# A list scheduler that lets ScalarE and VectorE read the same PSUM banks one after the other

## The chip, the cores and the metric

The kernel runs on one core of a Trainium2 chip. The metric is the device time of one execution in microseconds; the time before is 1328.19 us, the median of three runs (1327.75 to 1329.28).

## What is computed

12480 tokens of 128 channels go through an attention with 49 agents, then through two feed-forward blocks of 2048 hidden channels: the first with silu, the second with a rational function of its hidden value. All in float32; the weights come as float64 and are converted on the chip.

```python
a2k = softmax(agents @ k.T * scale)            # 49 x 12480
agent_v = a2k @ v                              # 49 x 128
x = softmax(q @ agents.T * scale) @ agent_v    # 12480 x 128
h = x @ moe_w_in;  x = (h * sigmoid(h)) @ moe_w_out
h = x @ moe2_w_in
P = a0 + a1 * h + a2 * h**2 + a3 * h**3
Q = 1 + |b0| * |h| + |b1| * h**2
out = (P / (Q + 1e-6)) @ moe2_w_out
```

## The kernel before, in words

The tokens are worked in 25 groups of 512 (the last has 192), a group's hidden channels in 8 pairs of 128-channel blocks. A step has a name, a group `g` and a pair `p`:

- First block: M1 (TensorE, 4 matmuls into an `h` tile of two PSUM banks), S1 (ScalarE, silu from there into an `s` tile), M2 (TensorE, 2 float32 matmuls, each shown as two in the trace, adding into `x2`). After eight pairs XS (VectorE) splits `x2` into `xh` and `xl`.
- Second block: M3 (TensorE, 6 matmuls into an `h` tile). Four steps read that tile: U (z = a3 h + a2; VectorE L550 for pairs 0 to 3, ScalarE L548 for pairs 4 to 7), W1 (VectorE L575, z = z h), W2 (VectorE L579, z = (z + a1) h) and AB (ScalarE L557, m = |h|). N and Q (GpSimd, L563 and L571) make the denominator from `m` in a `y` tile of two pairs; L and R (ScalarE, L584 and L587) turn it into its reciprocal by a logarithm and a sigmoid; G2 (VectorE L591) joins numerator and reciprocal; M4 (TensorE L600) adds up the output, O1 to O3 transpose and store it.
- The queries of two groups together: QT, QTc, QS, QM, QE, QN, QB, QBc, QBl; QT, QS and QB are TensorE's (8 transposes, 16 score matmuls, 8 transposes).
- Ahead of it: k, v, the query and the matrices are loaded by SP's queue in the order of the string `LOADS` (k, v, q; a digit or sign is one of 16 matrix pieces of 512 KB). For each k piece KT, KC, KS, then KV (ScalarE) and KM (VectorE) read the scores; X0 to X2 take the maximum over all 13 pieces; EX, ET, EC, AV follow for each piece, then F0 to F4 and V0 to V2. A matrix piece goes through C0 to C3 (C4, C5), from a `raw` buffer of which there are four.

What limits running ahead: three `h` slots, one `x2` and one `ot` bank, five `s`, thirteen `z`, two `m` and six `y` tiles. An activation table holds silu, logarithm, sigmoid or exponential, and a change is a table load; the four logarithms and four sigmoids of a group run as one batch in which no silu may start.

The order of every engine's instructions is fixed when the program is built. `scheduled` plays the kernel through with a length for each step (`COST`), a time that a result needs to another engine (`TELL`, `TAIL`), and a priority `g + place[0] + place[1] * p / 8` from `PLACE`; it takes on each engine, among the steps that could start within `SLACK` of the soonest, the one with the smallest number. The two readers U and AB of one `h` tile have no dependence on each other in this list: it may place them at the same time. The tile framework, which puts in the semaphores, lets no two engines use the same PSUM bank at once: of two readers on different engines, the second in the program's order waits for the first. An engine's queue is worked in order, so an instruction that waits holds up what stands behind it.

Of the kernel before, what the change touches and what calls it, by code (L numbers as in the profile page):

```python
# [26 lines left out]
NX = 1  # L27
NKV = 11

LOADS = "kkkkk0kkk1kkk2kqk3vv4vv5vv6vv7vv8vv9v:;<=>?"  # L30

# [16 lines left out]
}  # L48
PLACE = {
# [13 lines left out]
}  # L63
SLACK = {"PE": 0, "ACT": 0, "DVE": 0, "POOL": 3.73}
READY_Y = 4
TAIL = {"PE": 0.17, "ACT": 0.125, "DVE": 0.085, "POOL": 0.02, "DMA": 2.0}

# [4 lines left out]

TELL = {
    "PE": {"PE": -0.17, "ACT": 0.04, "DVE": 0.04}, "ACT": {"PE": 0.055, "DVE": 0.035, "POOL": 0.1, "ACT": 0.03},
    "DVE": {"PE": 0.055, "ACT": 0.095, "POOL": 0.1, "DVE": 0.02},
    "POOL": {"ACT": 0.1, "DVE": 0.1, "PE": 0.06, "POOL": 0.06}, "DMA": {"DMA": -2.0},
}
TABLE = {"S1": "silu", "L": "ln", "R": "sigmoid", "QE": "exp", "EX": "exp"}
SWITCH = 1.283

PORT = {"N", "Q", "G2", "QN", "C0", "C2", "C3", "C5"}
H_SLOTS = 3


def group_steps(groups, pairs, part=1.0):
# [16 lines left out]
    last, land = None, {}  # L102
    for i, what in enumerate(LOADS):
        n = count.get(what, 0)
# [101 lines left out]
def buf_counts(n=None):  # L206

    n = n or globals()
    return dict(
        h=n["H_SLOTS"], x2=1, ot=1, s=n["NS"], xh=n["NX"], z=n["NZ"], m=n["NM"], y=n["NY"], oT=1, ob=2,  # L210
        qT=1, e=1, xt=2, kv=NKV, raw=4, kT=2, eT=3, ca=2, cb=3, w2=2,
    )


def scheduled(groups, pairs, part=1.0):

    ops = group_steps(groups, pairs, part)
    bufs = buf_counts()
    free = {tag: [0.0] * n for tag, n in bufs.items()}
    taken = {tag: 0 for tag in bufs}  # L220
    users, last, where = {}, {}, {}
    waits, then = {}, {}
    for k, (_, _, after, _, uses, _) in ops.items():
        for t in uses:
            users[t] = users.get(t, 0) + 1
        waits[k] = len(after)
        for d in after:
            then.setdefault(d, []).append(k)
    at, end = {}, {}
    ready = {e: [] for e in TAIL}  # L230

    def becomes_ready(k):
        at[k] = max([end[d] + TELL[ops[d][0]].get(ops[k][0], 0.1) for d in ops[k][2]], default=0.0)
        ready[ops[k][0]].append(k)

    for k in ops:
        if not waits[k]:
            becomes_ready(k)
    idle = {e: 0.0 for e in TAIL}
    port = {"DVE": 0.0, "POOL": 0.0}  # L240
    table, batch = "exp", None
    n_ln, n_sig = {}, {}
    out = []

    def may_start(k):

        name, g, p = k
        eng, _, _, takes, _, _ = ops[k]
        t = max(idle[eng], at[k])
        for tag, _ in takes:  # L250
            held = free[tag] if tag == "h" else [free[tag][taken[tag] % bufs[tag]]]
            open_ = [x for x in held if x is not None]
            if not open_:
                return None
            t = max(t, min(open_))
        if name in TABLE and name != "R":
            if name == "L":
                if batch not in (None, g) or (batch == g and table != "ln"):
                    return None
                done = sum(all(("Q", g, 2 * h + i) in end for i in (0, 1)) for h in range(4))  # L260
                if batch is None and (p or done < READY_Y):
                    return None
            elif batch is not None:
                return None
        if name == "R" and n_ln.get(g, 0) < 4:
            return None
        if name in PORT:
            t = max(t, port["POOL" if eng == "DVE" else "DVE"])
        return t + (SWITCH if name in TABLE and TABLE[name] != table else 0.0)

    while len(out) < len(ops):
        best = None
        for eng, some in ready.items():
            can = [(t, k) for t, k in ((may_start(k), k) for k in some) if t is not None]
            if can:
                soon = min(can)[0] + SLACK.get(eng, 0.0)
                k = min((ops[k][5], t, k) for t, k in can if t <= soon)
                best = min(best or (1e9,), (k[1], k[0], k[2]))
        t, _, k = best
        name, g, p = k  # L280
        eng, cost, _, takes, uses, _ = ops[k]
        ready[eng].remove(k)
        idle[eng], end[k] = t + cost, t + cost + TAIL[eng]
        if name in PORT:
            port[eng] = max(port[eng], t + cost)
        slot = None
        for tag, what in takes:
            if tag == "h":
                i = slot = min(
                    (i for i, x in enumerate(free["h"]) if x is not None), key=lambda i: free["h"][i]  # L290
                )
            else:
                i = taken[tag] % bufs[tag]
                taken[tag] += 1
            where[what], free[tag][i] = (tag, i), None if users.get(what) else end[k]
        for what in uses:
            users[what] -= 1
            last[what] = max(last.get(what, 0.0), end[k] + 0.06)
            if not users[what] and what in where:
                tag, i = where[what]  # L300
                free[tag][i] = last[what]
        if name in TABLE:
            table = TABLE[name]
            if name == "L":
                batch, n_ln[g] = g, n_ln.get(g, 0) + 1
            elif name == "R":
                n_sig[g] = n_sig.get(g, 0) + 1
                batch = None if n_sig[g] == 4 else batch
        out.append((name, g, p, slot))
        for d in then.get(k, ()):  # L310
            waits[d] -= 1
            if not waits[d]:
                becomes_ready(d)
    scheduled.total = max(end.values())
    return out
# [3 lines left out]
def attention_silu_rational_kernel(  # L319
# [420 lines left out]
    def LD(i):  # L740
        what = LOADS[i]
        if what in "kv":
            load(*((k_t, k) if what == "k" else (v_t, v)))
        elif what == "q":
            q_load(0)
        else:
            job = ord(what) - 48
            load_w(matrices[job // NW], job % NW, job)
        if i == 2:
            nc.sync.dma_start(out=a_sb, in_=ca.partition_broadcast(P))  # L750
            nc.sync.dma_start(out=b_sb, in_=cb.partition_broadcast(P))
# [165 lines left out]
    for name, g, p, slot in scheduled(NG, NP, REST / GW):  # L917
        if late is None and name in ("AB", "U"):
            pre.close()
            late = ctx.enter_context(tc.tile_pool(name="late", bufs=2, reuse_waits="tile"))  # L920
        where = () if slot is None else (slot,)
        if name in steps:
            steps[name](g, p, *where)
        else:
            (one.get(name) or q_steps[name])(g, *where)
# [36 lines left out]
```

## Time and profile before

| | before |
|---|---|
| median of three runs | 1328.19 us |
| profiled execution, device time | 1329.12 us |
| its span | 1327.3 us |
| TensorE, matmuls busy | 1271.6 us (96%) |
| ScalarE busy | 1073.9 us (81%) |
| VectorE busy | 1005.3 us (76%) |
| GpSimd busy | 761.3 us (57%) |
| chain of work that ended last | PE 57%, DVE 23%, ACT 13%, issue 4%, DMA 2% |

The span is the stretch that the profile covers; the device time has 1.8 us around it. In the rows PE is TensorE, PEld its weight load, DVE VectorE, ACT ScalarE, POOL GpSimd, SPq the queue that issues DMAs. `L557` is line 557 of the kernel. A wait is put down to the instruction that released it. Matmuls overlap in the records, and their ends are modelled: a matmul of 0.23 us in the chain is listed with a duration of about 0.39.

### The profile page before, as it was taken

Reading aid. Unit: us, or ns where it says so; the run is one execution under the profiler, and the core shown is the slowest. Engines: PE = TensorE matmul, PEld = TensorE weight load, DVE = VectorE, ACT = ScalarE, POOL = GpSimd, SP = SyncE. Lnnn points to the kernel's source line nnn. Section 1 sums busy time; section 2 is a strip of 40 time slices with the busy share of each in tenths; the row PEclk is TensorE's granted clock in tenths of the full one; section 3 lists DMA queues with packets and bytes.
Section 4 is the critical chain, followed back from the end, with each engine's and each line's share of the span. In section 5 each row is a group of like instructions: output and inputs, shape, how many; then the busy total and the mean of one; then the engine's idle time right before and its main releaser. Section 6 shows DMA issues by size and latency. Waiting matters only on the chain.

```text
span 1327.3 us, 12283 instructions
## 1 busy us (share of the span) xinstructions
PE 1271.6 (96%) x4539; PEld 759.1 (57%) x4539; DVE 1005.3 (76%) x948; ACT 1073.9 (81%) x972; POOL 761.3 (57%) x434
## 2 busy tenths in 40 slices
PE   9899999999999999999999999999999999999987
PEld 5765565555555565565555555555555555555554
DVE  4987778858858787876867858868768769778775
ACT  7686888987996978888787887878878878869876
POOL 2247575556547575484466457556556466575672
PEclk9899999999999999999999999999999999999989
DMA  9720000000000000000000000000000000000000
GB/s 345 280 64 0 17 8 13 12 9 1 24 3 5 24 5 7 21 1 24 9 0 11 22 0 9 24 1 8 21 4 9 3 8 8 9 0 9 8 1 20
DMA packets 14676, 34.77 MB, mean 26 GB/s; under 512 B 1575, under 2 KB 5720, under 8 KB 14616
## 3 DMA queue, kind: packets, MB, share of 16 engines
q1 hardware_dynamic: 14616, 33.98, 7.0%
q8 instruction: 36, 0.59, 0.2%
q14 instruction: 24, 0.20, 0.0%
HBM read 27.59 MB, written 6.39 MB: 26 GB/s over the span
## 4 chain that ended last, share of the span: by engine, by line
PE 57%; DVE 23%; ACT 13%; issue 4%; DMA 2%; POOL 1%; SPq 0%; ACTq 0%; DVEq 0%; POOLq 0%
PE x L516 18%; PE ot L600 13%; DVE z L575 7%; DVE z L579 6%; DVE z L550 6%; PE h L502 5%; PE h L503 5%; PE h L539 5%; ACT m L557 4%; PE h L541 4%; PE h L540 4%; ACT y L584 3%; DVE z L591 3%; ACT z L548 3%; DMA s<-in_k_dram 1%
## 5 line engine op out<-in xcount | busy, mean ns | idle before, releaser
L563 POOL TENSOR_SCALAR y<-m,bab 128x1024 f32<-128x1024 f32 (+1 forms) x200 | 264.4, 1325 | 480.3 <-ACT m L557 462.9
L571 POOL TENSOR_TENSOR y<-y,m 128x1024 f32<-128x1024 f32 (+1 forms) x200 | 468.6, 2358 | 5.2
L516 PE MATMUL x<-s,wo 128*128 128x512 f32 (+1 forms) x800 | 361.9, 581 | 0.4 <-ACT s L509 0.4
L600 PE MATMUL ot<-z,w2o 128*128 128x512 f32 (+1 forms) x800 | 356.7, 588 | 4.4 <-ACT ob L626 2.3
L575 DVE TENSOR_TENSOR z<-z,h 128x1024 f32<-128x1024 f32 (+1 forms) x200 | 237.5, 1191 | 100.3 <-ACT m L557 58.6
L579 DVE SCALAR_TENSOR_TENSOR z<-z,a_sb,h 128x1024 f32<-128x1024 f32 (+1 forms) x200 | 249.5, 1252 | 38.8 <-ACT m L557 34.9
L591 DVE SCALAR_TENSOR_TENSOR z<-z,a_sb,y 128x1024 f32<-128x1024 f32 (+1 forms) x200 | 260.3, 1354 | 19.3 <-ACT y L587 16.6
L557 ACT ACTIVATE m<-h 128x1024 f32<-128x1024 f32 (+1 forms) x200 | 197.8, 1002 | 87.8 <-DVE z L550 44.5
L600 PEld LDWEIGHTS ot<-z,w2o 128*128 128x128 f32 x800 | 150.4, 191 | 159.4 <-issue 145.2
L509 ACT ACTIVATE s<-h 128x1024 f32<-128x1024 f32 (+1 forms) x200 | 196.9, 1004 | 52.1 <-PE h L503 50.0
L516 PEld LDWEIGHTS x<-s,wo 128*128 128x128 f32 x800 | 148.5, 189 | 127.6 <-issue 117.2
L539 PE MATMUL h<-xh,w2l 128*128 128x512 f32 (+1 forms) x400 | 187.1, 468 | 32.0 <-DVE z L579 24.3
L502 PE MATMUL h<-xt,w1a 128*128 128x512 f32 (+1 forms) x400 | 193.0, 484 | 2.7 <-DVE z L579 2.3
L584 ACT ACTIVATE y<-y,eps 128x2048 f32<-128x2048 f32 (+1 forms) x100 | 192.2, 1955 | 0.3
L587 ACT ACTIVATE y<-y 128x2048 f32<-128x2048 f32 (+1 forms) x100 | 181.1, 1862 | 0.3
L548 ACT ACTIVATE z<-h,a_sb 128x1024 f32<-128x1024 f32 (+1 forms) x100 | 118.4, 1184 | 67.9 <-PE h L541 54.2
L550 DVE TENSOR_SCALAR z<-h,a_sb 128x1024 f32<-128x1024 f32 (+1 forms) x100 | 131.1, 1313 | 37.6 <-PE h L541 27.1
L541 PE MATMUL h<-xh,w2h 128*128 128x512 f32 (+1 forms) x400 | 158.9, 397 | 0.0
L540 PE MATMUL h<-xl,w2h 128*128 128x512 f32 (+1 forms) x400 | 158.5, 396 | 0.0
L503 PE MATMUL h<-xt,w1b 128*128 128x512 f32 (+1 forms) x400 | 154.9, 388 | 0.0
L539 PEld LDWEIGHTS h<-xh,w2l 128*128 128x128 f32 x400 | 77.1, 193 | 97.5 <-issue 42.2
L502 PEld LDWEIGHTS h<-xt,w1a 128*128 128x128 f32 x400 | 75.3, 188 | 51.6 <-issue 15.2
(102 smaller groups left out, 866.0 us busy)
## 6 DMA issues: line engine op xcount, KB each, us to landing
q<-in_q_dram SPq DMA_DIRECT2D x12, 512.0 KB, 3.2
out_dram<-ob SPq DMA_DIRECT2D x24, 256.0 KB, 2.0
raw<-in_moe_w_in_dram SPq DMA_DIRECT2D x8, 512.0 KB, 8.7
raw<-in_moe_w_out_dram SPq DMA_DIRECT2D x8, 512.0 KB, 5.9
s<-in_k_dram SPq DMA_DIRECT2D x6, 512.0 KB, 6.5
kv<-in_k_dram SPq DMA_DIRECT2D x6, 512.0 KB, 9.9
s<-in_v_dram SPq DMA_DIRECT2D x6, 512.0 KB, 10.6
kv<-in_v_dram SPq DMA_DIRECT2D x6, 512.0 KB, 9.4
```

What stands on the lines that cost most here:

```text
L502: nc.tensor.matmul(h[:, c, :w], w1a[:, f], xt, start=True, stop=False)
L503: nc.tensor.matmul(h[:, c, :w], w1b[:, f], xt, start=False, stop=True)
L516: nc.tensor.matmul(x2_t[i][:, : cols(i)], wo[:, 2 * p + c, :], s[:, c, : cols(i)], start=(p == 0 and c == 0), stop=(p == NP - 1 and c == 1),)
L539: nc.tensor.matmul(h[:, c, :w], w2l[:, f], xh_t[i], start=True, stop=False)
L557: nc.scalar.activation(m, h2_t[i, p][:, :, : cols(i)], AF.Abs)
L563: nc.gpsimd.tensor_scalar(out=y_t[i, p // 2][:, p % 2], in0=m_t[i, p], scalar1=bab[:, 1:2], scalar2=bab[:, 0:1], op0=ALU.mult, op1=ALU.add,)
L571: eng.tensor_mul(out=y, in0=y, in1=m_t.pop((i, p)))
L575: nc.vector.tensor_mul(out=z, in0=z, in1=h)
L579: nc.vector.scalar_tensor_tensor(out=z, in0=z, scalar=a_sb[:, 1:2], in1=h, op0=ALU.add, op1=ALU.mult)
L584: nc.scalar.activation(y_t[i, h], y_t[i, h], AF.Ln, bias=eps)
L591: nc.vector.scalar_tensor_tensor(out=z, in0=z, scalar=a_sb[:, 0:1], in1=r, op0=ALU.add, op1=ALU.mult)
L600: nc.tensor.matmul(ot_t[i][:, : cols(i)], w2o[:, 2 * p + c, :], z[:, c, :], start=(p == 0 and c == 0), stop=(p == NP - 1 and c == 1),)
```

## The change

- Steps that read the same PSUM tile (`SHARED`: U, AB, W1, W2 of one group and pair; KV and KM of one k piece) are known to the list: a step may not start before the readers of the same tile on another engine have ended, plus the time to tell it. The list chooses other work in the meantime.
- The length of a table change, `SWITCH`, goes from 1.283 to 1.41; the time from the last use of a buffer to its next user from 0.06 to 0.11; `TELL` from VectorE to itself from 0.02 to 0.035.
- All priorities in `PLACE` and the slacks are others (GpSimd's from 3.73 to 10.19, ScalarE's and VectorE's from 0 to 0.1 and 0.11).
- `LOADS` has the k pieces ahead of nearly all else.

No step, tile, buffer count or instruction is changed. The diff, with the table of priorities cut to the steps that the text speaks of:

```diff
-LOADS = "kkkkk0kkk1kkk2kqk3vv4vv5vv6vv7vv8vv9v:;<=>?"
+LOADS = "kkkkkkkk0kkkk1qkv2v3vv4v5vv6v7vv8v9vv:;<=>?"
...
-    "M1": (-0.314, 1.025), "S1": (1.145, 0.916), "M2": (1.021, 0.1), "XS": (-6.422, 0),
-    "M3": (0.964, 0.941), "U": (2.183, 0.836), "W1": (-5.204, 0.983), "W2": (1.364, 0.136),
-    "AB": (2.549, 1.023), "N": (-2.99, 1.223), "Q": (-1.833, 1.4), "L": (5.032, 1.117),
-    "R": (1.379, 0.297), "G2": (1.461, 0.282), "M4": (2.885, 1.172), "O1": (-0.735, 0),
...
+    "M1": (-0.11, 0.763), "S1": (4.253, 0.495), "M2": (2.55, 0.413), "XS": (-10.282, 0),
+    "M3": (0.977, 1.183), "U": (0.653, 0.161), "W1": (2.726, 1.345), "W2": (-4.862, 0.973),
+    "AB": (-4.491, 0.498), "N": (-6.136, 0.226), "Q": (-3.0, 1.078), "L": (6.243, 0.379),
+    "R": (-3.253, 0.354), "G2": (1.443, 0.848), "M4": (4.598, 1.086), "O1": (-0.008, 0),
...
-SLACK = {"PE": 0, "ACT": 0, "DVE": 0, "POOL": 3.73}
+SLACK = {"PE": 0, "ACT": 0.1, "DVE": 0.11, "POOL": 10.19}
...
-    "DVE": {"PE": 0.055, "ACT": 0.095, "POOL": 0.1, "DVE": 0.02},
+    "DVE": {"PE": 0.055, "ACT": 0.095, "POOL": 0.1, "DVE": 0.035},
...
-SWITCH = 1.283
+SWITCH = 1.41
...
+SHARED = {"U": "h", "AB": "h", "W1": "h", "W2": "h", "KV": "k", "KM": "k"}
...
+    seen = {}
...
+        if name in SHARED:
+            for e, x in seen.get((SHARED[name], g, p), {}).items():
+                if e != eng:
+                    t = max(t, x + TELL[e].get(eng, 0.1))
...
+        if name in SHARED:
+            seen.setdefault((SHARED[name], g, p), {})[eng] = end[k]
...
-            last[what] = max(last.get(what, 0.0), end[k] + 0.06)
+            last[what] = max(last.get(what, 0.0), end[k] + 0.11)
```

## Rows read from the trace of the kernel before

**Rows 1.** Page, part 1: busy us (share of the span) xinstructions.
```profile
PE 1271.6 (96%) x4539; PEld 759.1 (57%) x4539; DVE 1005.3 (76%) x948; ACT 1073.9 (81%) x972; POOL 761.3 (57%) x434
```

**Rows 2.** Timeline of VectorE: XS of groups 1, 3, 11, 13 and 23 (start us, us).
```profile
132.02 0.69 DVE L529 CAST xh<-x 128x512 fp32r<-128x512 f32 x1 [2.83 <-PE x L516]
...
228.37 0.68 DVE L529 CAST xh<-x 128x512 fp32r<-128x512 f32 x1
...
624.26 0.69 DVE L529 CAST xh<-x 128x512 fp32r<-128x512 f32 x1 [5.64 <-PE x L516]
...
727.82 0.69 DVE L529 CAST xh<-x 128x512 fp32r<-128x512 f32 x1 [4.44 <-PE x L516]
...
1237.12 0.69 DVE L529 CAST xh<-x 128x512 fp32r<-128x512 f32 x1 [2.54 <-PE x L516]
```

**Rows 3.** Chain of work in order of time, three stretches: start us, us, what.
```profile
444.82 1.73 PE h L440 x16
...
472.99 0.23 PE h L502
...
475.32 1.72 PE x L516 x4
...
624.23 0.87 PE h L422 x8
```

**Rows 4.** Waits of the whole span, TensorE: us in total, times, longest us.
```profile
PE h L539 <- DVE z L579: 24.3, 27, 1.8
```

**Rows 5.** Waits of the whole span, ScalarE and VectorE on AB, U, W1 and GpSimd.
```profile
DVE z L575 <- ACT m L557: 58.6, 58, 2.5
...
ACT m L557 <- DVE z L550: 44.5, 30, 7.9
...
DVE z L579 <- ACT m L557: 34.9, 31, 1.2
...
ACT m L557 <- DVE z L575: 22.6, 35, 3.0
...
ACT m L557 <- POOL y L571: 9.6, 9, 1.2
```

**Rows 6.** Timeline of ScalarE, 629 to 641 us: [idle before <-releaser].
```profile
629.71 1.02 ACT L557 ACTIVATE m<-h 128x1024 f32<-128x1024 f32 x1 [0.93 <-DVE z L550]
...
637.64 1.03 ACT L557 ACTIVATE m<-h 128x1024 f32<-128x1024 f32 x1 [1.13 <-DVE z L550]
...
638.68 1.28 ACT L587 ACT_TABLE_LOAD   x1
...
639.98 1.91 ACT L587 ACTIVATE y<-y 128x2048 f32<-128x2048 f32 x1
```

**Rows 7.** Timeline of TensorE at the same hole.
```profile
641.38 0.47 PE L539 MATMUL h<-xh,w2l 128*128 128x512 f32 x1 [1.84 <-DVE z L579]
```

**Rows 8.** Chain of work in order of time, after the hole.
```profile
643.55 0.43 PE h L540
```

**Rows 9.** Timeline of ScalarE: two silus.
```profile
478.50 1.95 ACT L509 ACTIVATE s<-h 128x1024 f32<-128x1024 f32 x2
```

**Rows 10.** Timeline of VectorE: the last reader of a slot.
```profile
476.64 1.28 DVE L579 SCALAR_TENSOR_TENSOR z<-z,a_sb,h 128x1024 f32<-128x1024 f32 x1 [1.15 <-ACT m L557]
```

**Rows 11.** Chain of work in order of time: the next matmul in that slot.
```profile
477.98 0.50 PE h L502
```

**Rows 12.** Timeline of ScalarE: the first exponential.
```profile
36.16 0.71 ACT L833 ACTIVATE sT<-sT,mx 128x512 f32<-128x512 f32 x1
```

**Rows 13.** Busy us (xinstructions), granted clock and DMA of two stretches.
```profile
core 0: us, PE busy (x) PEld busy (x) DVE busy (x) ACT busy (x) POOL busy (x), PEclk, DMA share, GB/s
...
30.00:45.00 15.00, 11.07 (x72) 8.33 (x69) 13.59 (x29) 13.87 (x34) 4.19 (x3) 0.67 1.05 387
...
1237.00:1328.00 91.00, 74.14 (x277) 45.85 (x275) 64.67 (x68) 68.36 (x67) 46.90 (x34) 0.93 0.03 10
```

**Rows 14.** Waits of SP's queue: us in total, times, longest us.
```profile
SPq L668 <- DVE sb L706: 11.9, 3, 8.6
```

18 rows, old and new, of the table PLACE are left out of this document.

## The prediction

> **What bounds the kernel now.** I read the busy times of the page first [rows 1]. TensorE is busy for 96% of the span, so the kernel looks bound by matmuls with little to win. Ends of matmuls are modelled, though, so the busy share hides short holes. A better measure is the distance between two equal events. XS, the first reader of a finished `x2`, stands once in every group [rows 2]. From group 1 (132.02) to group 23 (1237.12) lie 1105.1 us for 22 groups, which is 100.5 us for two (the query work comes once in two groups). The first such pair, 132.02 to 228.37, took 96.4, a later one, 624.26 to 727.82, took 103.6.
>
> Against that I set what TensorE needs. In a stretch without holes one M1 and one M3 follow each other from 472.99 to 475.32: 2.33 us. M2 takes 1.72 [rows 3], and M4 has the same matmuls. Two groups have 16 pairs: 16 x (2.33 + 1.72 + 1.72) = 92.3. The query steps add 1.73 for QS and 0.87 for eight transposes, twice (QT and QB); O2 is four transposes, 0.44, twice. Together 92.3 + 3.5 + 0.9 = 96.7 us. The excess is 100.5 - 96.7 = 3.8 us in two groups, over eleven of them about 41 us. That is all that a better order can win between group 1 and group 23.
>
> Who makes these holes? Where TensorE stood still, the waits name M3 waiting for DVE L579 (W2), which is the last reader of an `h` tile [rows 4]: all three `h` slots are taken. So I looked at what keeps a slot. After M3, its two banks are read by U, AB, W1 and W2, and in the waits AB (ScalarE) and the three others (VectorE in half of the pairs, U on ScalarE in the other half) wait for each other again and again [rows 5]: 58.6 + 34.9 us on VectorE, 44.5 + 22.6 us on ScalarE, together 160.6 us in 154 waits for 200 pairs. None of these is a need of the data; AB shares nothing with U, W1 and W2 but the bank it reads. The scheduler of before knows nothing of it and places AB beside U, so the instruction that comes second stands at the head of its queue and holds up work that was ready.
>
> One hole shows it [rows 6]: within the logarithms of one group, AB at 629.71 held ScalarE up for 0.93 us until U was done, and AB at 637.64 for 1.13 us again. When M3 began at 641.38, TensorE had stood still for 1.84 us [rows 7], and soon after M3 ran with 0.43 us for a matmul instead of 0.23 [rows 3, 8], the lower of TensorE's two clock levels (1.2 GHz).
>
> **The change, part by part.**
>
> *Readers kept apart.* The removal is in the order, not in the chip's work: no instruction is added or taken away; the same four readers still go one after the other. What can vanish is the head-of-line wait. By the rows above, 160.6 us of such waits go with 41 us of holes: 0.26 us on TensorE for each. The waits on ScalarE (44.5 + 22.6 = 67 us) I take as gone: silu, logarithm and sigmoid work lies ready in most stretches, as around the two waits of the hole above. The waits on VectorE (93.5 us) I take as gone by a third, 31 us: before a sigmoid is done there is no G2, so VectorE often has nothing else. So 98 us x 0.26 = 25 us are won. The bounds: nothing (each wait is replaced by idling at another place), and 41 us (no hole left).
>
> *Two lengths.* A change of the activation table costs more than its own 1.28 us. AB at 637.64, table load, sigmoid at 639.98: 2.34 us from start to start [rows 6]; two silus take 1.95 together, so they stand 0.93 apart, since the second's own 1.02 closes them [rows 9]. So the change adds 1.41 us, which is the new value and not the old 1.283. That gives about 0.12 us, 87 times: 10 us of ScalarE's time that the list of before did not know of. The other length, from the last reader to the next matmul in the slot, goes from 0.06 to 0.11. In the trace W2 starts at 476.64 and ends 1.28 later, at 477.92; the next M1 starts at 477.98, but its first matmul takes 0.50 instead of 0.23 [rows 10, 11]. So the true price is 0.06 + 0.27 = 0.33 us, and the list stays 0.2 us short for each reuse that TensorE waits for. Both are errors of placing, no work; I give them no time of their own and keep them as a reason to stay well under the 41 us.
>
> The Trainium skill ("ScalarE: Activation LUTs", What ACT_TABLE_LOAD costs) puts a change of table at 1283 ns plus a drain of about 1380 ns, 2.66 us in all. The trace agrees on the first figure and not on the sum [rows 6, 9]. By the page the new length would still miss 1.25 us at each of 87 changes, and I would keep less of the gain; I go by the rows.
>
> *Priorities drawn anew.* Read from the table: AB becomes ScalarE's first choice (-4.491, was 2.549), silu stands behind it and U (4.253), W2 becomes VectorE's early choice, M1 and M3 stay ahead of M2, M4 stays last on TensorE. AB right after M3 means that a pair with U on VectorE has one hand-over instead of two, which fits the item above, where this is counted already. The slack of GpSimd grows from 3.73 to 10.19 us: it may stand idle that long for a more urgent step. It is busy for 57% of the span [rows 1] and sits behind ScalarE; AB waited for its Q only 9.6 us in 9 waits [rows 5], so I take nothing. If that cover goes, it is the rival below.
>
> *k first.* The thirteenth load of k moves from place 16 to 15 of the list, the twelfth from 14 to 12; v and the matrices 2 to 9 close up behind. The first exponential, which needs all scores, starts at 36.16, and between 30 and 45 us the DMA engines run at 387 GB/s with TensorE's clock at 0.67 of full speed [rows 12, 13]. A load of 0.52 MB is 1.35 us at that rate: scores are complete one load earlier, perhaps two. I take 2 us. Bounds: 5 us won if with it the stretch at half clock shortens by 10 us (15 us x 0.33 / 0.5 = 10 us at 1.2 GHz, half of which is lost), 5 us lost if the matrix loads, now closer together on four `raw` buffers, stall SP's queue: they waited for VectorE's conversion up to 8.6 us [rows 14], and every v behind them on SP waits too.
>
> *The end.* From XS of group 23 to the end 90 us pass, of which TensorE is busy 74 of 91 [rows 13]. The same head-of-line waits lie here; I take 2 us, bounds 8 won and 6 lost, since a different place of the last logarithms moves the whole chain.
>
> **The sum.** The profiled execution took 1329.12 us, 1327.3 of it span, 0.9 above the median of 1328.19. 1329.1 - 25 - 2 - 2 = 1300, and less 0.9 for the median: 1299. Rounded by the doubt on the slot's length: 1300.
>
> **Rivals.**
>
> *The holes are a lack of buffers.* Three `h` slots, five `s` and thirteen `z` tiles are what they were; while ScalarE does its four logarithms and four sigmoids, silu may not run, and TensorE must live on M2 and M4 from these buffers. Then the holes only move: 1329 less 0 to 4 us of start and end, 1325 to 1330. For it: where TensorE stands still, M3 waits for a slot [rows 4]. Against it: with the same buffers the pair from 132.02 took 96.4 us, as much as the work itself [rows 2]. The Trainium skill ("Perfetto Trace Analysis", Identifying the Most-Contended Engine) says that a gap repeating on the engine that should be saturated can mean too little SBUF or PSUM for the next tile; by that rule the time stays. The trace shows the repeating gap, but also shows it differing from pair to pair.
>
> *The order is right and the engines starve elsewhere (slower).* AB first on ScalarE needs an `m` tile, there are two, and Q on GpSimd frees them. If GpSimd now waits up to 10 us for a more urgent N, AB stands at the head of ScalarE's queue with U, silu and the logarithms behind it. The price by the same 0.26: the 98 us are not won, and each further 100 us of AB waiting for POOL costs 26 us. It decides against the change from about 110 us of such waits (now 9.6); at 200 us the time is 1329 + 25 = 1354, and a shorter start or end does not make up for that.
>
> *All holes go*, with the half-clock stretches that follow them: 1328 - 41 - 5 - 8 = 1274 at best, 1280 in the middle of this case.
>
> *It does not do what it says:* the list keeps readers apart on paper, but real lengths differ by more than the gaps it leaves (0.035 to 0.1 us), so second readers still wait. Then half of the 25 us: 1312 to 1325.
>
> **Chances.** The forecast (1285 to 1312) 0.56, all holes gone 0.10, half the gain 0.09; buffers or no change 0.11; slower 0.14. A measurement of this kernel tells about 0.2% (2.7 us) from no change. So faster 0.75, same 0.11, slower 0.14. The range leaves out about 0.06 below 1280 and 0.12 above 1333.
>
> **What would show it.** Right: the waits AB on U and W1 and W1, W2 on AB fall from 160.6 to some 60 us; XS of groups 1 and 23 stand about 1080 us apart; M3's wait for L579 falls. The first exponential starts at about 34. Wrong, if XS keeps 100 us for two groups though the reader waits are gone (buffers), if AB's waits for POOL L571 rise past 100 us, or if v is held up behind the matrix loads and the first silu comes later.

## The result and the profile after

The changed kernel took 1274.45 us (median of 4, 1273.71 to 1274.53), against 1328.29 for the kernel before beside it: a ratio of 0.959, 95% interval [0.958, 0.961]. The gain of 53.8 us is nearly twice the 29 us that were forecast, and the time lies below the range.

The busy times of the page, us (share of the span) x instructions. They answer to [rows 1].

```profile
PE 1246.6 (98%) x4539; PEld 763.1 (60%) x4539; DVE 989.4 (78%) x948; ACT 1069.1 (84%) x972; POOL 733.9 (58%) x434
```

From the busy share one would see two points on TensorE. The distance of equal events shows more. The timeline of VectorE, the XS of groups 1, 3, 11, 13 and 23, as in [rows 2]; lines have moved down by 9, so L529 is L538 now:

```profile
128.68 0.69 DVE L538 CAST xh<-x 128x512 fp32r<-128x512 f32 x1
...
222.74 0.69 DVE L538 CAST xh<-x 128x512 fp32r<-128x512 f32 x1 [1.74 <-PE h L550]
...
608.54 0.69 DVE L538 CAST xh<-x 128x512 fp32r<-128x512 f32 x1 [1.75 <-PE h L550]
...
705.00 0.69 DVE L538 CAST xh<-x 128x512 fp32r<-128x512 f32 x1 [1.50 <-PE h L550]
...
1184.53 0.69 DVE L538 CAST xh<-x 128x512 fp32r<-128x512 f32 x1 [0.78 <-PE h L550]
```

Group 1 to group 23 is now 1184.53 - 128.68 = 1055.85 us, was 1105.1. The pair 608.54 to 705.00 took 96.46, its counterpart of before 103.6. The profiled execution is 55.4 us shorter in its span (1271.9 against 1327.3): 3.3 of it before XS of group 1, 49.25 between the two, 2.8 behind (87.4 instead of 90.2).

One stretch of both kernels says the same by another view: 160 to 1180 us, busy us (x instructions) of PE, PEld, DVE, ACT, POOL, then TensorE's granted clock, DMA share, GB/s. First before, then after.

```profile
160.00:1180.00 1020.00, 993.91 (x3300) 584.30 (x3298) 776.85 (x672) 841.98 (x709) 605.08 (x324) 0.99 0.03 10
```

```profile
160.00:1180.00 1020.00, 1020.00 (x3472) 617.92 (x3470) 794.01 (x700) 878.74 (x743) 602.55 (x339) 1.00 0.03 11
```

TensorE has no idle time left in these 1020 us, and does 172 matmuls more in them. Before, it shows 26 us of holes in this stretch. The distance, over a stretch only a little longer, shows 49.25 us: part of a hole is hidden by the modelled ends, and matmuls at the lower clock count as busy too.

The waits on the four readers (us in total, times, longest us), which answer to [rows 4, 5]. U is L557 on ScalarE and L559 on VectorE, AB L566, W1 L584, W2 L588, M3 L548 to L550, Q L580:

```profile
DVE z L584 <- ACT z L557: 74.7, 49, 4.6
...
ACT m L566 <- DVE z L584: 38.3, 21, 1.8
...
DVE z L559 <- ACT m L566: 35.0, 26, 2.6
...
PE h L548 <- DVE z L588: 2.3, 3, 1.8
...
ACT m L566 <- POOL y L580: 1.1, 2, 0.6
```

Counting every wait between AB on one side and U, W1, W2 on the other, before has 168.2 us (160.6 of them in the four lines of [rows 5]) and after 73.5, nearly all in the second and third line here. U before W1 is a need of the data and stays. TensorE's wait for W2 at M3 has fallen from 24.3 to 2.3 us. The new order at work, within the logarithms of one group, first ScalarE, then VectorE (timeline; start and us of each):

```profile
618.22 2.01 ACT L593 ACTIVATE y<-y,eps 128x2048 f32<-128x2048 f32 x1
620.13 1.00 ACT L566 ACTIVATE m<-h 128x1024 f32<-128x1024 f32 x1
621.03 3.89 ACT L593 ACTIVATE y<-y,eps 128x2048 f32<-128x2048 f32 x2
624.82 1.00 ACT L566 ACTIVATE m<-h 128x1024 f32<-128x1024 f32 x1
625.72 2.00 ACT L593 ACTIVATE y<-y,eps 128x2048 f32<-128x2048 f32 x1
```

```profile
622.28 1.34 DVE L559 TENSOR_SCALAR z<-h,a_sb 128x1024 f32<-128x1024 f32 x1
623.66 1.22 DVE L584 TENSOR_TENSOR z<-z,h 128x1024 f32<-128x1024 f32 x1
624.91 1.28 DVE L588 SCALAR_TENSOR_TENSOR z<-z,a_sb,h 128x1024 f32<-128x1024 f32 x1
626.11 1.34 DVE L559 TENSOR_SCALAR z<-h,a_sb 128x1024 f32<-128x1024 f32 x1
```

AB (620.13, 624.82) stands between logarithms without an idle moment, and U, W1, W2 of a pair follow each other on VectorE with no ScalarE reader among them. In [rows 6] AB held ScalarE up twice, for 0.93 and 1.13 us.

### The profile page after: what moved, and what is told of

It reads as the page before. It is cut to its first block, busy times and chain, and to the rows that moved or that the text cites. A ratio compares the mean times of both kernels' runs of the same rounds, so it can differ in the third digit from the quotient of the medians.

```text
span 1271.9 us, 12354 instructions
## 1 busy us (share of the span) xinstructions
PE 1246.6 (98%) x4539; PEld 763.1 (60%) x4539; DVE 989.4 (78%) x948; ACT 1069.1 (84%) x972; POOL 733.9 (58%) x434
## 4 chain that ended last, share of the span: by engine, by line
PE 92%; DVE 4%; ACT 3%; issue 1%; ACTq 0%; DVEq 0%
PE ot L609 25%; PE x L525 25%; PE h L548 7%; PE h L550 7%; PE h L549 7%; PE h L511 7%; PE h L512 7%; PE h L449 2%; PE h L793 1%; PE h L484 1%; PE ot L629 1%; DVE z L584 1%; PE h L431 1%; ACT m L566 1%; PE x L867 1%
## 5 line engine op out<-in xcount | busy, mean ns | idle before, releaser
L572 POOL TENSOR_SCALAR y<-m,bab 128x1024 f32<-128x1024 f32 (+1 forms) x200 | 237.5, 1188 | 448.3 <-ACT m L566 444.7
L580 POOL TENSOR_TENSOR y<-y,m 128x1024 f32<-128x1024 f32 (+1 forms) x200 | 467.2, 2348 | 8.0
L609 PE MATMUL ot<-z,w2o 128*128 128x512 f32 (+1 forms) x800 | 362.6, 587 | 2.9 <-DVE z L600 2.2
L584 DVE TENSOR_TENSOR z<-z,h 128x1024 f32<-128x1024 f32 (+1 forms) x200 | 236.1, 1192 | 80.8 <-ACT z L557 74.7
L566 ACT ACTIVATE m<-h 128x1024 f32<-128x1024 f32 (+1 forms) x200 | 199.6, 998 | 106.6 <-PE h L550 66.2
L600 DVE SCALAR_TENSOR_TENSOR z<-z,a_sb,y 128x1024 f32<-128x1024 f32 (+1 forms) x200 | 239.6, 1263 | 38.4 <-ACT y L596 38.4
L588 DVE SCALAR_TENSOR_TENSOR z<-z,a_sb,h 128x1024 f32<-128x1024 f32 (+1 forms) x200 | 249.3, 1253 | 5.0
L518 ACT ACTIVATE s<-h 128x1024 f32<-128x1024 f32 (+1 forms) x200 | 192.4, 1004 | 29.3 <-PE h L512 24.0
L548 PE MATMUL h<-xh,w2l 128*128 128x512 f32 (+1 forms) x400 | 185.0, 462 | 6.8 <-ACT m L566 3.9
L511 PE MATMUL h<-xt,w1a 128*128 128x512 f32 (+1 forms) x400 | 188.7, 473 | 2.9 <-DVE z L588 2.6
L559 DVE TENSOR_SCALAR z<-h,a_sb 128x1024 f32<-128x1024 f32 (+1 forms) x100 | 131.4, 1314 | 36.2 <-ACT m L566 35.0
L550 PE MATMUL h<-xh,w2h 128*128 128x512 f32 (+1 forms) x400 | 156.9, 392 | 0.0
L557 ACT ACTIVATE z<-h,a_sb 128x1024 f32<-128x1024 f32 (+1 forms) x100 | 115.8, 1186 | 2.3 <-PE h L550 1.3
L548 PEld LDWEIGHTS h<-xh,w2l 128*128 128x128 f32 x400 | 76.0, 190 | 48.5 <-ACT s L518 18.0
## 6 DMA issues: line engine op xcount, KB each, us to landing
s<-in_v_dram SPq DMA_DIRECT2D x6, 512.0 KB, 10.1
```

Source lines behind the costliest of these rows:

```text
L511: nc.tensor.matmul(h[:, c, :w], w1a[:, f], xt, start=True, stop=False)
L548: nc.tensor.matmul(h[:, c, :w], w2l[:, f], xh_t[i], start=True, stop=False)
L550: nc.tensor.matmul(h[:, c, :w], w2h[:, f], xh_t[i], start=False, stop=True)
L572: nc.gpsimd.tensor_scalar(out=y_t[i, p // 2][:, p % 2], in0=m_t[i, p], scalar1=bab[:, 1:2], scalar2=bab[:, 0:1], op0=ALU.mult, op1=ALU.add,)
L580: eng.tensor_mul(out=y, in0=y, in1=m_t.pop((i, p)))
L584: nc.vector.tensor_mul(out=z, in0=z, in1=h)
```

## The experiments

The edits come in five sets: the bank conflict taken out by itself, the parts of the change, the lengths, the loads, and other priorities. "Distance" is from XS of group 1 to XS of group 23; "reader waits" are all waits between AB and U, W1, W2. "Holes" are the distance over after's 1055.85. "Planned" is the distance in the list's own plan, with the times that `scheduled` works out when the kernel is built; it comes from the kernel's text and not from a trace.

### Is it the shared bank?

The order of before, untouched, with AB reading a tile of SBUF instead of the bank:

```
-nc.scalar.activation(m, h2_t[i, p][:, :, : cols(i)], AF.Abs)
+src = w2h[:, : 2 * cols(i)].rearrange("p (h w) -> p h w", h=2).bitcast(F32)
+nc.scalar.activation(m, src, AF.Abs)
```

> The kernel before, its order untouched; only AB reads 1024 columns of the weights w2h in SBUF instead of the h tile (so m, and with it the denominator, is not the reference's). The second readers of a bank then have nobody to wait for. Theory 1, the holes come from reader waits: the 41 to 49 us between XS of group 1 and group 23 go, 1279 to 1290 us in all. Rival, lack of buffers: the h slot is still held by U, W1 and W2, whose lengths are the same, and the time stays within 1322 to 1330. Rival, the wrong length of a table change: it stays too, 1320 to 1330.

Measured: 1274.69 us, ratio 0.960 [0.958, 0.962]. XS of groups 1 and 23 in the timeline:

```profile
129.82 0.69 DVE L529 CAST xh<-x 128x512 fp32r<-128x512 f32 x1 [2.43 <-PE x L516]
...
1184.53 0.69 DVE L529 CAST xh<-x 128x512 fp32r<-128x512 f32 x1 [2.71 <-PE x L516]
```

The distance is 1054.7 us: by this measure the old order has no holes once AB is out of the bank. The gain is 53.2 us, against 53.8 for the whole change, with the same buffers, priorities and lengths. The edit frees more than the readers: AB no longer waits for M3, and it no longer holds the tile. But in before AB waited for M3 (PE L541) only 8.1 us in 12 waits, against 168.2 for the readers, and TensorE's matmuls waited for AB as the last reader of a tile only 2.9 us in 2 waits.

The same for half of the pairs: 0 to 3, whose U is on VectorE, and 4 to 7, whose U is on ScalarE.

```
+if p not in U_ACT:   # second kernel: if p in U_ACT
+    src = w2h[:, : 2 * cols(i)].rearrange("p (h w) -> p h w", h=2).bitcast(F32)
```

> The kernel before, order untouched; AB of pairs 0 to 3 alone, where U is on VectorE, reads weights in SBUF (the denominator is not the reference's). If holes come from both kinds of pair alike: half of the 53 us, about 1301 us. If pairs with U on VectorE make them (AB on U was the longest wait): 1280 to 1290.

> The kernel before, order untouched; AB of pairs 4 to 7 alone, where U is on ScalarE, reads weights in SBUF (the denominator is not the reference's). Both kinds alike: about 1301 us. If pairs with U on VectorE make the holes: 1315 to 1325. If the two gains add up, this one and that of pairs 0 to 3 make 53 us together; if a hole needs both, less.

Measured: 1290.55 (0.972 [0.971, 0.974], distance 1070.2) and 1312.98 (0.989 [0.987, 0.990], 1091.3). The gains, 37.9 and 15.4 us, add up to 53.3, the whole. The pairs in which AB and U sit on different engines make 70% of the loss.

The changed kernel with AB out of the bank tells what its remaining 73.5 us of reader waits cost:

> The changed kernel, its order untouched; only AB reads weights in SBUF instead of the h tile (so the denominator is not the reference's). Theory 1, waits that the list planned cost nothing: 1270 to 1275 us, though 73 us of reader waits go. By the rate of the prediction they would be worth 19 us: 1255.

Measured: 1271.82, ratio 0.957 [0.955, 0.958], distance 1056.15. The waits are gone and the distance stays. At most 2.6 us hang on 73.5 us of waits (and on the 66.2 us that AB waits for M3 in after, which the edit takes away too), and the two intervals overlap.

### The parts of the change

Before with the new knowledge alone (of the `h` tiles; KV and KM are left out), old priorities and lengths:

```
+SHARED = {"U": "h", "AB": "h", "W1": "h", "W2": "h"}
+if name in SHARED:
+    for e, x in seen.get((SHARED[name], g, p), {}).items():
+        if e != eng:
+            t = max(t, x + TELL[e].get(eng, 0.1))
```

> The kernel before with one part of the change: the list knows that U, AB, W1 and W2 of one tile exclude each other. Old priorities, old lengths, old order of loads. Theory 1 (what the list does not know is what hurts): most of the gain, 1280 to 1300 us. Rival, the priorities make the gain: 1320 to 1340. The rate of the prediction (0.26 us for each us of reader wait, whoever knows of it) gives 1300 if half of the waits go.

Measured: 1299.65, 0.979 [0.977, 0.981]; reader waits 55.2 us, distance 1072.65. The waits fall further than in after, yet 17 us of holes stay and the end takes 100.2 us instead of 87.4. The holes are in the plan already, which has 1070 us.

Before with the new PLACE and SLACK alone:

> The kernel before with the new priorities and slacks alone: the list knows nothing of shared banks, the lengths and the order of loads are the old ones. Theory 1: the list again plans second readers into a busy bank, so no gain to speak of, 1315 to 1345 us. Rival, the priorities make the gain (AB first on ScalarE): 1275 to 1290.

Measured: 1350.24, 1.018 [1.016, 1.020]. Reader waits 137.6 us, distance 1119.65. The new priorities under the old knowledge are worse than the old ones, by more than was expected.

Before with the three new lengths alone:

> The kernel before with the three new lengths alone: no knowledge of shared banks, old priorities, old loads. Theory 1: the reader waits stay near 168 us, and so do the holes, 1315 to 1345 us. If the wrong lengths were a cause of their own: 10 us or more faster, 1300 to 1318.

Measured: 1314.42, 0.989 [0.987, 0.990]. Reader waits have grown to 195.4 us, and yet the distance is 21 us shorter than before's, 1083.9. The time lies in the range of the second case, but the expectation for the waits missed: what the lengths won here, they did not win by fewer waits.

After without the knowledge, everything else new (`SHARED = {}`):

> The changed kernel, but its list does not know that readers of one bank exclude each other; priorities, lengths and loads are the new ones. Theory 1 (unknown waits hurt, known ones do not): as with the new priorities alone, the stretch between XS of groups 1 and 23 grows from 1056 to 1085 or more, 1300 to 1350 us in all, with reader waits over 110 us. The rate of the prediction (0.26 us of hole for each us of reader wait, known or not): the kernel changed has 73.5 us of such waits and no holes, so this rate would give under 1290 for 137 us.

Measured: 1307.68, 0.984 [0.982, 0.985]; distance 1087.0, reader waits 161.7 us. Two rows of the waits:

```profile
DVE z L559 <- ACT m L566: 88.9, 43, 3.7
...
ACT m L566 <- DVE z L584: 51.9, 21, 3.7
```

So the knowledge is worth 28.6 us with old priorities and lengths (1328.2 to 1299.65) and 33.2 with new ones (1307.68 to 1274.45). The three parts do not add: alone they give -28.6, +22 and -13.8 us, together -20.4, where the whole change gives -53.8 (the loads, its fourth part, are below). Knowledge with the old priorities and the new lengths cannot be drawn (the list finds no step that may start), so what the priorities and the lengths give apart from each other, once the list has the knowledge, stays open.

The prediction's own explanation of the new priorities was AB first. That one entry in before:

```
-"AB": (2.549, 1.023)
+"AB": (-4.491, 0.498)
```

> The kernel before with AB's priority alone as in the changed kernel: AB becomes ScalarE's first choice right after M3. The prediction held that a pair then has one hand-over instead of two. If that is what helps: reader waits under 110 us and 1290 to 1315 us. Theory 1 (the list still plans AB and U into the same bank at the same time): reader waits stay over 110 us and the time within 1310 to 1345.

Measured: 1313.01, 0.989 [0.988, 0.991], the first case at its upper end. Reader waits halve, 168 to 87 us, but the distance falls by 21.5 only, to 1083.6: 28 us of holes stay.

### The lengths

After with all three old lengths (the change of table, the reuse of a slot, and VectorE's step to its own next one):

```
-SWITCH = 1.41
+SWITCH = 1.283
-"DVE": 0.035   and   end[k] + 0.11
+"DVE": 0.02    and   end[k] + 0.06
```

> The changed kernel with the three old lengths (table change 1.283, reuse 0.06, VectorE to itself 0.02). If the lengths matter as the 10 us of unknown table time say: 5 to 15 us slower, 1279 to 1290. If only the shared banks matter: 1272 to 1277. Over 1300 would mean that the priorities fit one set of lengths alone.

Measured: 1328.3, ratio 1.000 [0.999, 1.001]: the whole gain is gone. XS of groups 1 and 23, and the largest reader wait:

```profile
125.93 0.69 DVE L538 CAST xh<-x 128x512 fp32r<-128x512 f32 x1 [0.57 <-PE h L550]
...
1229.18 0.69 DVE L538 CAST xh<-x 128x512 fp32r<-128x512 f32 x1 [0.57 <-PE x L525]
```

```profile
DVE z L559 <- ACT m L566: 73.3, 30, 3.7
```

The distance is 1103.25. It could be lateness (the list short by 0.1 us at 87 places, so that readers wait after all) or just another order, drawn worse. Four kernels bear on this. First two of the lengths, one at a time (the reuse alone wasn't set back):

> The changed kernel with one length set back: the list takes 1.283 us for a change of table instead of 1.41. Theory 1 (what the plan does not know makes the holes): ScalarE falls behind the plan by about 0.45 us in each group (3.5 changes of 0.127), so holes come back in the stretch between XS of groups 1 and 23: 1285 to 1320 us in all. If the wrong length of a table change is too small to matter: 1272 to 1278.

> The changed kernel with another length set back: 0.02 instead of 0.035 us between two dependent steps on VectorE. It is 0.015 us, about 0.5 us in a group. If size is what counts: 1272 to 1280. If the priorities fit one plan only and any redrawing loses it, the loss sits in few groups and the rest keeps 96.5 us for two groups: 1285 to 1310.

Measured: 1276.82 (0.962 [0.961, 0.964]) and 1299.54 (0.979 [0.977, 0.980]). The list that doesn't know of 10 us of ScalarE's time gives a kernel 2.4 us slower, and the intervals touch. The 0.015 us of VectorE cost 25 us, and the timeline shows where: XS of groups 1, 3 and 23.

```profile
125.78 0.68 DVE L538 CAST xh<-x 128x512 fp32r<-128x512 f32 x1
...
235.89 0.69 DVE L538 CAST xh<-x 128x512 fp32r<-128x512 f32 x1 [1.36 <-PE h L550]
...
1195.80 0.68 DVE L538 CAST xh<-x 128x512 fp32r<-128x512 f32 x1
```

The first two groups took 110.1 us instead of 94.1 and the stretch behind XS of group 23 103.6 instead of 87.4; all other pairs of groups took 94 to 96.5, as in after. A lateness of 0.015 us would be spread over all groups. This is a different drawing that is bad at two places, and both stand in its plan: 107.6 us for the first two groups (91.9 in after's plan) and 96.6 behind XS of group 23 (83.6).

Then real lateness with the order kept: copies of one column on ScalarE, unknown to the list, ahead of the first logarithm and the first sigmoid of each group, one or ten.

```
+if h == 0:
+    nc.scalar.copy(first, eps)      # second kernel: for _ in range(10)
```

> The changed kernel, its order untouched; ahead of the first logarithm and the first sigmoid of each group stands a copy of one column on ScalarE that the list does not know of, 50 in all, about 0.2 us each, 0.4 us in a group. It is the same lateness as a table change that is reckoned too short, without a redrawn order. Theory 1: holes come back, 1280 to 1300 us. If the order alone carries the gain and bears some lateness: 1273 to 1277, no more than the 10 us that the copies take.

> The changed kernel, order untouched, with ten copies of one column on ScalarE ahead of the first logarithm and the first sigmoid of each batch: 500 that the list does not know of, about 0.1 us each when queued, 2 us in a group, 50 us in all. If the order bears lateness of that size: under 1285 us. If holes follow unplanned lateness: 1295 to 1330.

Measured: 1273.9 (0.960 [0.958, 0.961], so no change from after) and 1350.5 (1.016 [1.015, 1.018]). The groups of the page for the first, and for the second with ten: instructions, busy us, mean ns, idle us before them.

```profile
L599 ACT COPY first<-eps 128x1 f32<-128x1 f32 x25 | 5.0, 200 | 0.0
L594 ACT COPY first<-eps 128x1 f32<-128x1 f32 x25 | 4.8, 193 | 0.0
```

```profile
L601 ACT COPY first<-eps 128x1 f32<-128x1 f32 x250 | 48.2, 193 | 7.1
L595 ACT COPY first<-eps 128x1 f32<-128x1 f32 x250 | 47.9, 192 | 7.1
```

The order bears 0.4 us of lateness in each of 25 groups for nothing. About 4.4 us in each (96 us of copies and 14 of idling, by 25) cost 76 us, two thirds of it. The copies took twice the length that was expected, and the time lies above both ranges: a lateness of this size isn't borne.

Last, the order with the old lengths with AB out of the bank, to see whether its holes are reader waits:

> The changed kernel with the three old lengths, order as drawn from them; only AB reads weights in SBUF instead of the h tile (the denominator is not the reference's). If its holes (1103 us between XS of groups 1 and 23) are bank waits that the plan places wrongly: that stretch falls to 1056 to 1070 and the whole to 1280 to 1295 us. If the order itself is poor or the table changes make it late: it stays at 1090 or more, 1315 to 1330 us.

Measured: 1322.35 (1314.41 to 1326.22), 0.995 [0.993, 0.997], distance 1094.2. Without any reader wait it keeps 38 of its 47 us of holes, so bank waits are not what makes most of them. The order as it was planned accounts for 11 us only: the plan has 1066 us, where the chip took 1103. A candidate stands in the trace. GpSimd's N and VectorE's G2, which the list keeps apart, take 1374 and 1474 ns here on the mean, in after 1188 and 1263. Played again in its own order with these longer steps, the plan of old_len comes to some 1099 us; after's order, with the same steps as long, to 1059. That is a calculation and not a run: what starves TensorE in this order stays open.

### The loads

After with the old order of loads:

```
-LOADS = "kkkkkkkk0kkkk1qkv2v3vv4v5vv6v7vv8v9vv:;<=>?"
+LOADS = "kkkkk0kkk1kkk2kqk3vv4vv5vv6vv7vv8vv9v:;<=>?"
```

> The changed kernel with the old order of loads. If k first is worth what lies between the starts of the two kernels (the first silu came 2 to 3 us earlier): 1276 to 1279 us. If nothing: 1274. If the whole later order hangs on how the start is drawn, anything from 1270 to 1300.

Measured: 1282.0, 0.966 [0.964, 0.967], more than k first was expected to be worth. The distance is after's (1056.3), so the 7.6 us are the start; in the profiled execution, which took 1284.3, XS of group 1 came 10.1 us later. The first silu:

```profile
77.98 1.94 ACT L518 ACTIVATE s<-h 128x1024 f32<-128x1024 f32 x2
```

It stands at 68.87 in after, but also at 69.22 in before, which has these same old loads. So these loads cost the changed kernel 9 us up to the first silu, while in before the first silu comes no later for them. Before with the new loads alone cannot be drawn either.

### Other priorities

Knowledge and lengths kept, PLACE, SLACK and LOADS searched for anew, twice, to see whether the one set of the change is special and whether a faster one is near:

> The changed kernel with priorities, slacks and the order of loads drawn anew once more under the same knowledge and lengths; its loads mix k with the first matrix pieces and the query (kkk0kk1kkkkkkkqk23v4vv...). If a plan that knows the banks is kept by the chip: XS of groups 1 and 23 stand 1055 us apart again, XS of group 1 comes 3 to 5 us earlier, 1268 to 1272 us in all. If priorities of the changed kernel were suited to the chip beyond the plan: 1280 or more.

> A second redrawing, with another order of loads (kkkkk0kkkkkkk1qk234vv5v...) and AB behind W2 and U in the priorities of VectorE and ScalarE. If a plan that knows the banks is kept by the chip, whichever reader comes first: 1054 us between XS of groups 1 and 23 and 1268 to 1273 us in all. If AB first is what makes the changed kernel fast: 1285 or more.

Measured: 1273.88 (0.958 [0.956, 0.960]) and 1283.51 (0.965 [0.964, 0.967]). The first equals after: distance 1055.25, XS of group 1 at 125.65 (3 us earlier, with k mixed among the matrices), its end 3.8 us longer. The second has a distance of 1061.8. Both are slower than was expected. The second, with AB behind W2 and U, stays below the 1285 that would have spoken for AB first, but is 9 us slower than after. No version was clearly faster than after, and two other sets of priorities came to the same distance or near it.

## Why the prediction was wrong

**What bounds it: right.** The distance of equal events, the readers of one bank and the head-of-line waits were the right reading; nobank_before shows it with the order untouched. Only the need was set a little high. I worked out 96.7 us for two groups; in after nine of the eleven pairs take 96.4 to 96.5 and the first and last 94.1 and 93.65. So not 41 us could be won between group 1 and group 23 but at least 49.

**Readers kept apart: the step that failed.** "160.6 us of such waits go with 41 us of holes: 0.26 us on TensorE for each", and then "98 us gone, 25 us won". The number of waits was nearly right: I expected them to fall to some 60 us, they fell to 73.5 in all (38.5 in the kinds of [rows 5]). The rate was near right for the waits of before and wrong for those that stay, which I had cost 62 x 0.26 = 16 us; no single rate would have done. Of the 24 us between my 25 and the measured 49, these 16 are the step that failed, and the other 8 are the need that was set too high. Reader waits and holes of the runs:

| kernel | list knows the bank | reader waits, us | planned, us | distance, us | holes, us |
|---|---|---|---|---|---|
| after | yes | 73.5 | 1055.2 | 1055.85 | 0 |
| redrawn11 | yes | 95.3 | 1055.2 | 1055.25 | -0.6 |
| redrawn14 | yes | 99.2 | 1053.5 | 1061.8 | 6 |
| old_tell | yes | 57.7 | 1068.9 | 1070.0 | 14 |
| share_only_h | yes | 55.2 | 1070.1 | 1072.65 | 17 |
| old_len | yes | 108.8 | 1066.1 | 1103.25 | 47 |
| ab_first | no | 86.6 | 1056.9 | 1083.6 | 28 |
| len_only | no | 195.4 | 1049.6 | 1083.9 | 28 |
| no_share | no | 161.7 | 1055.2 | 1087.0 | 31 |
| before | no | 168.2 | 1050.6 | 1105.1 | 49 |
| place_only | no | 137.6 | 1081.5 | 1119.65 | 64 |

In after 73.5 us of waits are worth at most 2.6 us, 0.04 for each (nobank_after); at my rate they would be 19. In before 168.2 us are worth the whole 49, 0.29 for each (nobank_before). What separates these two, whose orders were held, is whether the list has the wait in its plan: after's plan holds some 80 us of such waits itself, and its distance is 1055.2 with them. Over the table the same holds: a list that doesn't know of the bank missed its own plan by 27 to 55 us, one that does by no more than 8.3, except in old_len, by 37. How a wait that the list doesn't know turns into a hole (by holding up silu, or the last reader of a slot) was followed at one hole only [rows 6, 7]. I had counted the waits as if all were alike. That share_only_h, with 113 us of waits less, came out 28.6 us faster, as my rate would have it, is luck: its holes are planned ones.

**Two lengths: one misread, and wrong as a reason to stay under 41.** The table's 1.41 us stands [rows 6, 9]. The slot's 0.33 us does not. I set the 0.50 of the first matmul, from its own start to its end, against 0.23, which is the distance of one matmul from the next [rows 3, 11]. The timeline of TensorE in before lists an undisturbed matmul with 0.39 too:

```profile
477.98 0.50 PE L502 MATMUL h<-xt,w1a 128*128 128x512 f32 x1
478.32 0.39 PE L503 MATMUL h<-xt,w1b 128*128 128x512 f32 x1
478.55 0.39 PE L502 MATMUL h<-xt,w1a 128*128 128x512 f32 x1
```

From start to start the first takes 0.34 instead of 0.23. The price is 0.06 + 0.11 = 0.17 us, and the list with 0.11 is 0.06 short and not 0.2. After has no holes in spite of it, as late50 would lead one to expect. The prediction named lateness as the channel. Lateness of this size is borne (late50), and the 25 us of old_tell come from an order drawn anew, in ways that the size of the correction doesn't tell; for the 54 us of old_len the cause is open.

**Priorities: half right.** AB's entry alone gives 15 us (ab_first), with half of the reader waits gone; that "one hand-over instead of two" does it isn't shown, since len_only gains as much with more waits. Alone the whole set is slower by 22 us, so it doesn't pay without the knowledge. GpSimd's slack was rightly taken at nothing: AB's wait for Q fell from 9.6 to 1.1 us.

**k first: right in the transfer, wrong in what it frees.** The last load of k was issued at 15.75 instead of 17.11 us, 1.36 earlier, one load as worked out. But the first exponential came later, and I had set it at about 34:

```profile
37.04 0.71 ACT L842 ACTIVATE sT<-sT,mx 128x512 f32<-128x512 f32 x1
```

It was 36.16 [rows 12], and what delayed it is open. The bound that I named came in part: the clock was granted higher from 30 to 45 us, 0.89 instead of 0.67 [rows 13]. But the first silu came only 0.35 us earlier. Of the 3.3 us that are gained by XS of group 1, 3.0 lie behind the first silu, in a place that I had not described; that the sum is near the 2 that I took is luck. The window in after:

```profile
30.00:45.00 15.00, 11.78 (x102) 9.50 (x102) 13.46 (x31) 13.48 (x34) 2.91 (x3) 0.89 0.94 345
```

**The end: right in size**, 2.8 us for the 2 taken. In nobank_before this stretch takes 88.7 us, so the readers account for 1.5 of it.

**The rivals.** Lack of buffers fell: six kernels come to a distance of 1054.7 to 1056.3 us with the same buffers (after, nobank_before, nobank_after, old_loads, late50 with 1055.6, redrawn11). GpSimd starving AB fell by the 1.1 us above. Half the gain (the list keeps readers apart on paper only) fell too: after keeps its planned distance to 0.7 us. "All holes go" came true, and at the number that I gave as its best (1274), there by luck: its terms were 41, 8 and 5 us, and 49.25, 2.8 and 3.3 came. It got a chance of only 0.10, because my own rate spoke against it. Yet the pair 132.02 to 228.37 [rows 2], with 96.35 us, had shown the work itself being reached in the kernel before; that row was a better guide than the mean rate, though the same pair takes 94.1 in after and so had holes too. The Trainium skill ("PSUM — Partial Sum Buffer", PSUM bank collisions raise a hardware error) says that reads of one bank by ScalarE and VectorE must be kept apart by semaphores. In the traces they are: AB overlaps U, W1 or W2 of its tile in none of the 200 tiles, in before and in after. The runs show the price to lie in where those waits fall in an order fixed beforehand. The rule on repeating gaps that the prediction quotes stands in the Trainium skill under "Perfetto Trace Analysis", Optimization Strategy.

## What to carry to other kernels

In an order that is fixed beforehand, look for waits that the semaphores enforce and the planner doesn't know: here they cost little where they were planned and much where they were not. Don't turn the total of such waits into time by a mean rate; look for a stretch in which the bound engine already runs without a hole, take that as the floor, and give its case a large chance when the change tells the planner the missing rule. And a change that makes a greedy list draw anew can move the time by tens of microseconds for a length of hundredths: compare such parts with the order held fixed, as by taking the shared resource away, and set the plan's own time beside the chip's: it tells a poor plan from one that isn't kept.

## What the runs showed of the hardware

In after the loop's stretches at the lower clock (1.2 GHz) are gone with its holes. Before, the granted clock fell in four stretches of 3.4 us between 147 and 954 us, as behind the hole of [rows 7, 8]; the window there:

```profile
643.50:647.00 3.50, 3.50 (x9) 2.21 (x8) 3.50 (x4) 3.50 (x3) 0.00 (x0) 0.62 0.01 2
```

In after there is none between 157 and 1235 us, as the 1.00 over 160 to 1180 shows. But holes don't always bring one: old_len, with 47 us of holes, has none between 153 and 1278 us either.

```profile
160.00:1180.00 1020.00, 994.08 (x3349) 592.91 (x3348) 809.14 (x673) 847.19 (x713) 615.52 (x330) 1.00 0.03 10
```

Some steps of GpSimd and VectorE take longer where they run beside each other. In before the 160 N without a G2 beside them take 1187 ns on the mean, the other 40 take 1878; the 176 G2 without a Q beside them take 1254, the other 24 take 2086. In after only 6 N and 4 G2 have such a neighbour (groups of the page, x instructions, busy us, mean ns):

```profile
L572 POOL TENSOR_SCALAR y<-m,bab 128x1024 f32<-128x1024 f32 (+1 forms) x200 | 237.5, 1188 | 448.3 <-ACT m L566 444.7
...
L600 DVE SCALAR_TENSOR_TENSOR z<-z,a_sb,y 128x1024 f32<-128x1024 f32 (+1 forms) x200 | 239.6, 1263 | 38.4 <-ACT y L596 38.4
```

Over all 200, before has 1325 and 1354 ns, old_len 1374 and 1474. It need not cost anything: nobank_before still has 1351 and 1356 ns and is as fast as after. In old_len it may be what costs (The lengths).
